# Moving the output of a fused convolution and expert kernel onto TensorE, with squares as small products and some sums on GpSimd

## The chip, the cores and the metric

One core of a Trainium2 chip runs the whole program. The metric is the device time of one execution in microseconds (us), smaller is better. The kernel before takes 186.46 us (median of 4 runs, 184.03 to 187.41). Executions of one kernel differ: the 59 of before in the set of fw_best2 took 182.97 to 194.24 us. A run is called slow here when it lies over 1.5% above the fastest of the same kernel, and fast otherwise.

Engines are named as in the profile: PE is TensorE's matmuls, PEld its weight loads, DVE is VectorE, ACT ScalarE, POOL GpSimd, SP the queue that issues most transfers.

## The reference, cut to what matters

Two residual blocks on x of 2048 tokens by 640 features (five blocks of 128 features; sixteen tiles of 128 tokens). The first is a layer norm, a short and a long convolution (by FFT), and a product. The second is a layer norm, a routing score per token, and a gated expert on the eight best tokens alone.

```python
h = layernorm(x) * (1 + ca) + sa
x = x + ga * (h * y)                  # y: the convolutions of k, v
# ---- from here on: the tail ----
h = layernorm(x) * (1 + cb) + sb      # needs mean and variance of each token's row
r = h @ w_r                           # routing score, one per token
idx = argsort(-r)[:8]                 # eight tokens
hs = h[idx]
y = (silu(hs @ w_gate) * (hs @ w_up)) @ w_down * sigmoid(r[idx])
x = x + gb * (h + scatter(y, idx))    # output: every token; the expert's part: eight
```

With z = x·s − µ·s (s the reciprocal deviation, µ the mean), the output of an ordinary token is x + z·(gb(1+cb)) + gb·sb.

## The kernel before

The whole kernel is a list of steps in a hand-written order (`ORDER`); a star behind a step's name sends its PSUM evictions to DVE instead of ACT. The steps that the change touches, cut:

```python
def t_P(b):                                  # products and sums in frequency space
    ...
    V.tensor_tensor(out=T2[:], in0=X, in1=Hi, op=ALU.mult)
    V.tensor_tensor(out=X, in0=X, in1=Hr, op=ALU.mult)
    V.tensor_tensor(out=Xr, in0=Xr, in1=T2[:, :, 1, :], op=ALU.subtract)
    V.tensor_tensor(out=Xi, in0=Xi, in1=T2[:, :, 0, :], op=ALU.add)
    ...
def t_BT(b): ...    # inverse transform on PE, evicted to U, stored to DRAM (Ud)
def t_LU(b): ...    # loaded back in another layout (uA)
def t_AT(b):        # last factor on PE, product with h, "row addition" into xq
    ...
    V.tensor_tensor(out=t, in0=ps, in1=h, op=ALU.mult)
    V.tensor_tensor(out=xq[:, :, cc], in0=xq[:, :, cc], in1=t[:], op=ALU.add)
def t_S():          # squares of feature blocks 0 to 3, on ACT
    nc.scalar.activation(out=junk, in_=xq[:, m, 0:512], func=ACT.Square, accum_out=...)
def t_BS():         # base = x + gb*sb, formed on PE with the identity
    nc.tensor.matmul(ps[:, i, :], lhsT=ident[:], rhs=gbs[:, 0:512], start=True, stop=False)
    nc.tensor.matmul(ps[:, i, :], lhsT=ident[:], rhs=xq[:, 2 * j + i, 0:512], start=False, stop=True)
    evac(base, ps)
def t_R(b):         # transposes of xq, evicted to xT, products with w_r and with ones
    ...
def t_N():          # z of each tile: 5 on DVE, 11 on ACT
    nc.scalar.activation(out=xn(m), in_=xq[:, m, :], func=ACT.Identity, scale=rs2, bias=nm2)
def t_F():          # output: two DVE instructions for a pair of tiles
    V.tensor_tensor(out=x2, in0=xn(2 * j, 2), in1=gbo, op=ALU.mult)
    V.tensor_tensor(out=x2, in0=x2, in1=base, op=ALU.add)
def t_COL():        # columns of the modulation: transposes, eleven short DVE steps,
    ...             # then a product with ones that PE waits for (near 80 us)
def t_T():          # variance, score r_bf, top 8, one-hot, selected rows xsT,
    ...             # gate, up, down, delta, scatter onto the output
```

## Time and profile before

| | before |
|---|---|
| time, median | 186.46 us |
| span of the profiled run | 183.9 us |
| last row addition into xq ends | 147.03 us |
| score r_bf ends | 156.6 us |
| selected rows xsT end | 170.3 us |
| mean granted PE clock | 0.919 |

I cut the span by three events: the last row addition, the score r_bf, the end. The stretch to the first is called the front (147.0 us), the next the score (9.6 us), the last the tail (27.3 us). Of the page, two rows matter here; each digit is a fortieth of the span, PE's busy share and PE's granted clock in tenths:

```profile
PE   0669989985989999939999969999679578165850
PEclk9999999999999999995799999999999999955555
```

PE works nearly without a stop until three quarters of the span, stops once near 80 us (the 3), and in the tail works in pieces and at half clock (the 5s).

### The profile page before, as it was taken

What the parts mean: (1) busy time and instruction counts of PE and PEld (TensorE: products, weight loads), DVE (VectorE), ACT (ScalarE), POOL (GpSimd) and SP (SyncE); (2) the same over time, 40 slices, a digit from 0 to 9 for tenths busy, and PEclk for the clock granted to TensorE, in tenths of its full rate; (3) what the DMA queues carried; (4) which work ended last, traced back from release to release, by engine and by line L of the source; (5) the groups of instructions that cost most, each with busy time, mean ns of one, the idle gap of its engine ahead of it and who ended that gap; (6) DMA issues with size and microseconds to landing.
All of it is one profiled execution on the core that took longest, in us unless ns stands there. A gap on an engine that the chain in (4) does not pass through costs nothing.

```text
span 183.9 us, 4109 instructions
## 1 busy us (share of the span) xinstructions
PE 144.0 (78%) x1664; PEld 112.5 (61%) x1664; DVE 157.7 (86%) x283; ACT 136.2 (74%) x180; POOL 33.2 (18%) x81
## 2 busy tenths in 40 slices
PE   0669989985989999939999969999679578165850
PEld 0225979952768679837679759998577342024840
DVE  5869998988979899977599999989979996999930
ACT  4368789792897979775599979999448999996000
POOL 7997500005001022010010020020200102100003
PEclk9999999999999999995799999999999999955555
DMA  6999989999999999992041999994768099705540
GB/s 108 152 204 278 313 186 326 272 198 274 265 292 320 338 304 309 176 200 114 0 171 61 212 320 324 368 338 183 200 261 224 8 293 362 310 4 219 207 153 2
DMA packets 68668, 40.68 MB, mean 221 GB/s; under 512 B 44904, under 2 KB 64808, under 8 KB 68648
## 3 DMA queue, kind: packets, MB, share of 16 engines
q1 hardware_dynamic: 65160, 35.15, 72.7%
q0 software_dynamic: 1520, 5.25, 7.7%
q10 hardware_dynamic: 1968, 0.01, 0.7%
q8 instruction: 13, 0.21, 0.5%
q14 instruction: 7, 0.06, 0.1%
HBM read 24.67 MB, written 10.50 MB: 191 GB/s over the span
## 4 chain that ended last, share of the span: by engine, by line
DVE 27%; DMA 27%; PE 24%; ACT 12%; issue 6%; SPq 2%; POOLq 1%; POOL 0%; DVEq 0%; ACTq 0%
DMA kT<-in_A_k_dram 9%; PE ps L295 8%; ACT junk L404 7%; DMA kvd<-kvT 7%; DMA uA<-Ud 6%; DVE kvT L297 4%; DVE st L581 4%; PE ps L274 3%; PE ps L314 3%; DVE xq L641 3%; DMA Ud<-U 3%; DVE xq L643 3%; PE ps L384 2%; ACT U L58 2%; ACT A L58 2%
## 5 line engine op out<-in xcount | busy, mean ns | idle before, releaser
L58 ACT CAST A<-ps 128x1024 bf16<-128x1024 f32 x35 | 33.6, 1030 | 8.5 <-PE ps L274 8.5
L58 ACT CAST HX<-ps 128x1024 bf16<-128x1024 f32 x37 | 35.9, 1054 | 2.8 <-PE ps L318 2.8
L314 PE MATMUL ps<-A,FT 128*128 128x256 bf16 x160 | 36.2, 272 | 0.4 <-DVE kvT L297 0.4
L318 PE MATMUL ps<-A,FT 128*128 128x128 bf16 x160 | 35.0, 219 | 0.0
L316 PE MATMUL ps<-A,FT 128*128 128x128 bf16 x160 | 35.0, 219 | 0.0
L295 PE MATMUL ps<-kT,dg 128*128 128x512 bf16 x80 | 21.6, 426 | 7.0 <-DMA kT<-in_A_k_dram 7.0
L58 ACT CAST U<-ps 128x1024 bf16<-128x1024 f32 x20 | 19.8, 1048 | 5.0 <-PE ps L350 2.3
L295 PEld LDWEIGHTS <-dg 128*128 128x128 bf16 x80 | 8.5, 108 | 17.4 <-issue 3.8
L354 POOL DMA_DIRECT2D Ud<-U x10 | 5.7, 572 | 72.9 <-ACT U L58 62.9
L348 PE MATMUL ps<-IT,HX 128*128 128x256 bf16 x80 | 18.1, 273 | 0.8 <-DVE kvT L297 0.8
L350 PE MATMUL ps<-IT,HX 128*128 128x256 bf16 x80 | 18.1, 273 | 0.0
L297 DVE TENSOR_TENSOR kvT<-ps,vT 128x1024 bf16<-128x1024 f32 x10 | 12.1, 1220 | 6.9 <-PE ps L295 5.7
L318 PEld LDWEIGHTS <-FT 128*128 128x128 bf16 x160 | 15.7, 98 | 1.8
L316 PEld LDWEIGHTS <-FT 128*128 128x128 bf16 x160 | 15.6, 98 | 0.9 <-issue 0.8
L314 PEld LDWEIGHTS <-FT 128*128 128x128 bf16 x160 | 15.7, 98 | 0.3
L237 POOL TENSOR_SCALAR dg<-ident,shk_f 128x128 bf16<-128x128 bf16 x16 | 10.3, 659 | 20.0 <-PE ps L295 20.0
L384 PE MATMUL ps<-RAT,uA 128*128 128x128 bf16 x160 | 10.4, 219 | 4.2 <-DMA uA<-Ud 4.2
L404 ACT ACTIVATE junk<-xq 128x512 bf16<-128x512 bf16 (+1 forms) x23 | 12.2, 533 | 2.0 <-DVE xq L391 1.3
L389 DVE TENSOR_TENSOR t<-ps,h 128x1024 bf16<-128x1024 f32 x10 | 12.2, 1218 | 1.7 <-PE ps L384 1.6
L581 DVE BATCH_NORM_STATS2 st<-xq 128x6 f32<-128x320 bf16 x32 | 13.2, 478 | 0.5 <-DMA xq<-in_A_q_dram 0.5
L274 PE MATMUL ps<-RA,gA 128*128 128x256 bf16 x80 | 12.3, 309 | 1.5 <-DVE gA L281 1.5
L333 DVE TENSOR_TENSOR HX<-HX 128x2048 bf16<-128x2048 bf16 x10 | 12.2, 1225 | 0.4
(218 smaller groups left out, 308.6 us busy)
## 6 DMA issues: line engine op xcount, KB each, us to landing
Ud<-U POOLq DMA_DIRECT2D x10, 512.0 KB, 6.0
uA<-Ud SPq DMA_DIRECT2D x10, 512.0 KB, 6.5
early<-in_w_mod_dram SPq DMA_DIRECT2D x6, 800.0 KB, 7.3
gA<-in_A_ssm_k_dram SPq DMA_DIRECT2D x5, 512.0 KB, 5.0
kvd<-kvT SPq DMA_DIRECT2D x10, 256.0 KB, 3.9
xq<-in_A_q_dram SPq DMA_DIRECT2D x4, 640.0 KB, 6.4
xA<-kvd SPq DMA_DIRECT2D x5, 512.0 KB, 4.8
out_dram<-xq SPq DMA_DIRECT2D x4, 640.0 KB, 3.1
```

Source lines behind the costliest of these rows:

```text
L58: self.nc.scalar.copy(out=out, in_=in_)
L274: nc.tensor.matmul(ps[:, bb // 2, :, (bb % 2) * 8:(bb % 2) * 8 + 8], lhsT=src[:, 4 * g4 + bb, :], rhs=RA[:].rearrange("p k c e -> p (k c) ...
L295: nc.tensor.matmul(ps[:, i, :], lhsT=diags[b][:, j, :], rhs=kT[:, n0 - j:n0 - j + 512], start=(j == 0), stop=(j == 3))
L297: V.tensor_tensor(out=kvT[:, 1024 * i2:1024 * i2 + 1024], in0=ps[:].rearrange("p a b -> p (a b)"), in1=vT[:, 1024 * i2:1024 * i2 + 1024], ...
L314: nc.tensor.matmul(ps[:, i], lhsT=FT[:, 0, k2, :], rhs=A[:, 2 * k2:2 * k2 + 2, u, :], start=True, stop=False)
L316: nc.tensor.matmul(ps[:, i, 0, :], lhsT=FT[:, 1, k2, :], rhs=A[:, 2 * k2 + 1, u, :], start=False, stop=False)
L318: nc.tensor.matmul(ps[:, i, 1, :], lhsT=FT[:, 2, k2, :], rhs=A[:, 2 * k2, u, :], start=False, stop=True)
L348: nc.tensor.matmul(ps[:, i, :], lhsT=hx[:, k2, 0, 1, :], rhs=IT[:, k2, 1:3, :].rearrange("p a b -> p (a b)"), start=True, stop=False)
L350: nc.tensor.matmul(ps[:, i, :], lhsT=hx[:, k2, 1, 1, :], rhs=IT[:, k2, 0:2, :].rearrange("p a b -> p (a b)"), start=False, stop=True)
L384: nc.tensor.matmul(o, lhsT=uA[:, bb, cs * P:(cs + 1) * P], rhs=RAT[:, cs, :].rearrange("p (m e) -> p m e", e=8), start=(cs == 0), stop=(cs ...
L404: nc.scalar.activation(out=junk()[:, 0:n], in_=xq[:, m, b0 * P:b0 * P + n], func=ACT.Square, accum_out=dst[:, m:m + 1])
L581: V.bn_stats(out=st1[:, m, hf, :], in_=xq[:, m, hf * 320:hf * 320 + 320])
```

## The change

The intent: in the tail DVE and ACT did all the output work while PE had gaps, so the output goes to PE. The transposed rows, which the score needs anyway, are kept, and the output of a tile is five products of them with diagonal matrices diag(gb(1+cb)) plus two products of four rows (mean and deviation, each in two bf16 parts, against four rows of constants). The squares of blocks 0 to 3 become 32x32 products of the transposed rows with themselves, whose diagonal is picked out. Eleven large DVE sums go to POOL, the row sum is split from its product, the inverse root has two steps fewer, and the order string is new from its first line on.

```diff
-LK0 START TC RA DIAG0 RA TAB0 RAT LG0 LK1 C0:2 ...          (ORDER, rewritten as a whole)
+LK0 START RA LG0 RA DIAG0 TAB0 LK1 TAB0 TAB1 C0:2 TC ...
...
+    def off():
+        return nc.gpsimd if evac.vector else V
...
-            V.tensor_tensor(out=Xr, in0=Xr, in1=T2[:, :, 1, :], op=ALU.subtract)
-            V.tensor_tensor(out=Xi, in0=Xi, in1=T2[:, :, 0, :], op=ALU.add)
+            off().tensor_tensor(out=Xr, in0=Xr, in1=T2[:, :, 1, :], op=ALU.subtract)
+            off().tensor_tensor(out=Xi, in0=Xi, in1=T2[:, :, 0, :], op=ALU.add)
...
-    def t_S(): ...          (squares of blocks 0 to 3 on ACT)
-    def t_BS(): ...         (base on PE; t_BL likewise)
+    def t_GR():
+        ...
+                    for b in range(4):
+                        nc.tensor.matmul(ps[t, m, :], lhsT=xTs[b][:, m, t], rhs=xTs[b][:, m, t],
+                                         start=(b == 0), stop=(b == 3), tile_position=(0, 32 * j))
...
-    def t_N(): ...          (z on DVE and ACT)
     def t_F():
-            V.tensor_tensor(out=x2, in0=xn(2 * j, 2), in1=gbo, op=ALU.mult)
-            V.tensor_tensor(out=x2, in0=x2, in1=base, op=ALU.add)
+            for b in range(NB):
+                nc.tensor.matmul(ps[:, b * P:b * P + P], lhsT=xTs[b][:, m, :], rhs=dgb[:, b, :], ...)
+            nc.tensor.matmul(ps[:, 0:512], lhsT=h_["rows"][:, m, :], rhs=st4[:, 0, 0:512], ...)
+            nc.tensor.matmul(ps[:, 512:D], lhsT=h_["rows"][:, m, :], rhs=st4[:, 0, 512:D], ...)
+            (7 tiles)  V.scalar_tensor_tensor(out=o, in0=ps[:, 0:D], scalar=rs2, in1=xq[:, m, :], ...)
+            (9 tiles)  nc.scalar.mul(out=o, in_=ps[:, 0:D], mul=rs2); V.tensor_tensor(out=o, in0=o, in1=xq, ...)
```

## The prediction

> **What bounds the kernel now.** I read the page first, then the busy time of each engine by stretches, then the chain of waits in order of time, then the groups of instructions by shape, then single stretches of the timeline. On the page no engine is alone at its limit:
>
> ```profile
> PE 144.0 (78%) x1664; PEld 112.5 (61%) x1664; DVE 157.7 (86%) x283; ACT 136.2 (74%) x180; POOL 33.2 (18%) x81
> DVE 27%; DMA 27%; PE 24%; ACT 12%; issue 6%; SPq 2%; POOLq 1%; POOL 0%; DVEq 0%; ACTq 0%
> ```
>
> The shares differ by stage, so I cut the span at events of the chain of waits: 147.0 us is the end of the last addition into the rows xq, 153.4 us the start of the variance chain, 156.6 us the routing score r_bf, 170.4 us the selected rows. The stretches (columns: length, then busy us of PE, weight load, DVE, ACT, POOL, then clock, DMA share, GB/s):
>
> ```profile
> 20.00:80.00 60.00, 54.97 (x568) 44.92 (x566) 55.13 (x95) 48.73 (x55) 7.99 (x16) 1.00 1.09 272
> 80.00:90.00 10.00, 7.20 (x30) 4.50 (x31) 6.53 (x19) 6.31 (x7) 1.08 (x4) 0.66 0.44 112
> 90.00:130.00 40.00, 37.79 (x464) 33.75 (x462) 38.31 (x46) 35.23 (x37) 3.59 (x7) 1.00 0.74 229
> 147.00:153.40 6.40, 5.00 (x48) 2.88 (x49) 5.16 (x19) 6.05 (x25) 0.25 (x2) 1.00 0.94 304
> 156.60:170.40 13.80, 5.79 (x90) 3.66 (x90) 13.21 (x35) 12.06 (x15) 0.95 (x2) 0.66 0.46 177
> 170.40:184.00 13.60, 6.41 (x212) 5.98 (x212) 5.88 (x14) 0.35 (x2) 1.56 (x1) 0.50 0.33 115
> ```
>
> From 20 to 130 us DVE is 92 to 96% busy with ACT close behind: both empty PSUM, and PE waits for them. The exception is 80 to 90 us, where PE stops and comes back at half clock. From 138.3 to 153.4 us the chain is the squares on ACT, one after another; from 156.7 us it is DVE, and then the write of the output. In the chain of waits and the groups:
>
> ```profile
> 82.61 0.14 POOL early L525
> 82.80 0.59 PE ps L527 x2
> 83.61 4.38 PE ps L274 x20
> ...
> 152.99 0.41 ACT junk L404 x2
> 153.43 0.19 DVE tot L653
> ...
> 173.59 0.75 DVE xq L641
> 175.21 3.58 DMA out_dram<-xq
> L404 ACT ACTIVATE junk<-xq 128x512 bf16<-128x512 bf16 x16 | 10.1, 630 | 1.8 <-DVE xq L391 1.3
> L643 DVE TENSOR_TENSOR xq<-xq,base 128x1280 bf16<-128x1280 bf16 x8 | 6.6, 825 | 0.3
> L391 DVE TENSOR_TENSOR xq<-xq,t 128x1024 bf16<-128x1024 bf16 x10 | 6.9, 692 | 0.3
> ```
>
> [...] the 128x16 sum on POOL (L281) took 0.26 us at 45.5 us, but 1.24 us at 68.7 us, ending just after the DVE product L333 that ran from 68.57 to 69.79 us. [...] Here PE lay idle 79.9 to 82.8 us, the clock was 0.50 to 89 us, and after the idle stretch around 159 us it stayed 0.50 to the end. [...] The trace: 1.22 us from PSUM (L389), 0.69 us from SBUF, same 1024 columns.
>
> **The change, part by part.** The order of instructions on the engines shows what moved; durations are those of before.
>
> Front, to the last addition. Five pairs of spectral sums go to POOL: DVE loses 10 x 0.69 = 6.9 us, [...]. One of ten row sums goes too, -0.7. Two of the ten products after AT are split, copy on ACT (1.05) and product in SBUF (0.69), saving 2 x 0.5 = 1.1 on DVE. Against this DVE takes two more evictions, 2 x 1.21 = +2.4. DVE: -6.3 us; ACT: two evictions fewer, two copies more, zero. About 0.7 of it counts, since PE and ACT are near their limits too: -4.5. The memset of the ones moves to the start, so PE at 80 us no longer waits for POOL, though still for the eleven DVE instructions before L527, which end at 81.9 us: about 1 us of the stop goes, and with it perhaps the half clock, which cost about half of 6.6 us. I take -2.5 for both. The three evictions of base on DVE (3 x 1.22) leave the stretch 130 to 147 us, but that stretch waits for the round trip of the last block through DRAM (eviction ends 132.6, product starts 143.4): -1.5. The last store goes through SP instead of POOL: -1. [...] Sum: -7.
>
> From the last addition to r_bf (9.6 us before). The sixteen 512-wide squares (16 x 0.75 with the read of the accumulator = 12 us) leave ACT, and the base matmuls leave PE. In their place 256 small 32x32 matmuls. The 128x8 pairs of the expert stage run one per 26.7 ns (70 in 1.87 us), so I take 27 ns: 192 before the last block's transposes = 5.2 us, 64 after = 1.7 us. PE starts them about 2.6 us before the last addition, so the transposes slip about 2.5 us; then the eviction of the fifth block 1.2, mask product and reduction 0.7 each, two small ones: the variance starts about 6 us after the last addition instead of 6.4. The inverse root has 13 instead of 15 steps of 0.21 us: -0.4. Sum: -1.
>
> From r_bf to the end (27.3 us before). Gone: five normalisations on DVE and eleven on ACT (0.83 us apart, which the selection waited for) and sixteen DVE output instructions of 0.82 us. New: sixteen 4-column transposes (0.9 us warm, 1.7 cold), their copy on ACT (as xT, 1.87 us), and for each of sixteen row tiles 1280 PE columns: 0.55 us warm, 1.07 cold. Each tile is emptied by one DVE instruction from PSUM (0.85 us, seven tiles) or by ACT (0.75) plus a DVE sum (0.49, nine tiles). The path: r_bf, rows and top-8 in parallel until about +5, two output tiles, one-hot at about +6.5, selection directly from xq without waiting for the normalised rows (80 x 27 ns), scale and shift: the selected rows at about +10.5 instead of +13.7. But then PE has ten output tiles ahead of the gate matmuls, paced by ACT at 0.75 us; gate, four tiles and up follow on the same PE. The last tile lands in SBUF at about +21, the down product ends at about +24, the output write takes 3.7, and the closing scatter and end 5.1 (178.8 to 183.9 now). That makes about 29.8, or +2.5. The tail loses on its own: output and experts now share PE, where before DVE wrote the output while PE did the experts.
>
> Sum: -7 - 1 + 2.5 = -5.5, a span of 178.4 us. The profiled run took 1.8 us more than its span and the median 2.8 more, so I add 2.3: about 180.5 us.
>
> **Rivals.** (a) The front does not shorten: POOL's sums [...] block DVE fully, and what DVE is spared comes back as blocked products; [...]. For it: L281 at 68.7 us. Against it: the pairs have other blocks' work around them. Then the front gives -2, and the time is about 186. (b) PE stays at half clock through the output: 16 x 0.5 = 8 us more on PE, perhaps 5 on the path. For it: 0.50 from 161 us on in the present tail. Against it: from the selection on PE is now dense. Time about 184. (c) The reorder is worth more than I count: with loads in order of need and no PE stop, the front loses 11 us or more; the time is 174 to 176. For it: the order string was rewritten as a whole. (d) The small matmuls cost 50 ns a pair, so that the 192 take 9.6 us: +4 before the score, about 184.
>
> **Range and chances.** (a), (b) and (d) pull up to 184 to 187, (c) down to 174; with all three terms off by two or three us in either way I take 174.5 to 186.5. Faster by over 2% means under 183.0: 0.64. Within 2%: 0.31. Slower: 0.05, since it needs two rivals at once.
>
> **What would show it.** Right: the last row addition at 140 us (134 to 144); [...] no clock loss near 80 us; the variance chain about 6 us after the last addition; selected rows 10 to 11 us after the score; from score to end 29 to 31 us, longer than now. Wrong: a last addition later than 145 us, or a tail after the score of 27 us or less (then PE and ACT overlap better than I think), or above 33 (half clock).

## The result, and the profile after

The kernel after takes 201.06 us (median of 4 runs, 198.70 to 202.84). A ratio in this text is the mean time of one kernel's fast runs over that of the other's fast runs of the same rounds, so it is not quite the ratio of the medians quoted. It is 1.075 here, 95% interval 1.053 to 1.097: slower by 7.5%. The profiled run is slow (span 201.1 us); its clock, 0.852, is close to that of the fast runs (0.859 and 0.853), and the run without POOL sums, below, has a fast profile with the same tail. The spans of the fast runs are 196.8 and 198.5 us; less a tail of 41.1 us that leaves 155.7 to 157.4 us up to r_bf, by this estimate as much as before (156.6). So the tail carries nearly the whole loss between fast runs, and the +2.4 and +1.0 of the table belong to a slow one.

| | before | after | change | predicted |
|---|---|---|---|---|
| front, to the last row addition | 147.0 | 149.4 | +2.4 | −7 |
| score, to r_bf | 9.6 | 10.5 | +1.0 | −1 |
| tail, to the end | 27.3 | 41.1 | +13.8 | +2.5 |
| span | 183.9 | 201.1 | +17.2 | −5.5 |

The same rows of the page after, with the line of busy times that answers to the one in the prediction:

```profile
PE 161.0 (80%) x2007; PEld 124.2 (62%) x2010; DVE 149.6 (74%) x269; ACT 118.5 (59%) x141; POOL 68.5 (34%) x108
PE   0779998959999997089999999956872168999980
PEclk9999999979999999859999999999699555555555
```

DVE has 8 us less to do and ACT 18 us less, and yet the span is longer. PE's row ends in 8999980 above a clock of 5: it is full and slow. The tail by stretches (length, then busy us of PE, PEld, DVE, ACT, POOL, then clock, DMA share, GB/s):

```profile
149.40:160.00 10.60, 2.85 (x113) 2.44 (x112) 7.56 (x32) 2.82 (x14) 7.59 (x11) 0.77 0.66 214
160.00:172.30 12.30, 9.23 (x125) 6.54 (x125) 6.85 (x27) 1.91 (x2) 1.40 (x4) 0.50 0.01 1
172.30:192.50 20.20, 20.20 (x217) 10.78 (x216) 8.86 (x15) 7.49 (x11) 0.00 (x0) 0.50 0.27 99
```

For 20.2 us PE is busy without a gap, and the clock is 0.50 throughout. DVE and ACT stand idle more than half of that time: PE alone is the bound. One output tile on PE, from the timeline (start, duration, engine, line, operation, partitions of operands, shapes):

```profile
181.46 0.71 PE L672 MATMUL ps<-dgb,xT 128*128 128x128 bf16 x5
182.11 0.60 PE L674 MATMUL ps<-st,rows 4*128 4x512 bf16 x1
182.51 0.31 PE L675 MATMUL ps<-st,rows 4*128 4x128 bf16 x1
182.75 0.71 PE L672 MATMUL ps<-dgb,xT 128*128 128x128 bf16 x5
```

From one tile to the next is 182.75 − 181.46 = 1.29 us, where the prediction had 0.55 warm and 1.07 cold. The cold figure was right for products that fill all 128 rows, as a tile at the same clock of 0.50 shows in a later run, fw, in which the four rows are padded with zeros to 128:

```profile
172.08 0.74 PE L675 MATMUL ps<-dgb,xT 128*128 128x128 bf16 x5
172.61 0.63 PE L677 MATMUL ps<-st,rows 128*128 128x512 bf16 x1
173.04 0.31 PE L678 MATMUL ps<-st,rows 128*128 128x128 bf16 x1
173.14 0.74 PE L675 MATMUL ps<-dgb,xT 128*128 128x128 bf16 x5
```

Here it is 173.14 − 172.08 = 1.06 us. The products last about as long; most of the 1.29 − 1.06 = 0.23 us more in after lies where the number of rows changes: from the first of five products to the 512-column one 0.65 against 0.53 us, and from the last product to the next tile 0.24 against 0.10.

Near 80 us the timeline of after shows what POOL's sums do to DVE:

```profile
79.58 0.48 DVE L507 TENSOR_TENSOR modv<-modv 128x640 bf16<-128x640 bf16 x1
79.83 2.20 POOL L361 TENSOR_TENSOR HX<-HX,T 128x1024 bf16<-128x1024 bf16 x1 [3.26 <-DVE HX L359]
79.98 2.40 DVE L508 TENSOR_TENSOR modv<-modv 128x640 bf16<-128x640 bf16 x1
82.00 2.36 POOL L362 TENSOR_TENSOR HX<-HX,T 128x1024 bf16<-128x1024 bf16 x1
...
82.68 2.02 DVE L521 TENSOR_TENSOR modv<-modv 128x640 bf16<-128x640 bf16 x1
...
86.08 0.56 PE L536 MATMUL ps<-red,onesf 128*128 128x2 f32 x2 [7.04 <-DVE junk L533]
```

Products of the same shape take 0.48 us alone and 2.40 and 2.02 us beside a POOL sum. Of the eleven POOL sums of this run ten took 2.11 to 2.49 us and one 3.19 (at 109.8 us); on DVE the same sum took 0.69 us in before. PE waits for the end of that chain, 7.0 us where before it was 2.9. The bracket gives the idle time ahead of an instruction and what ended it.

Last, PE stops twice in the middle of a group of instructions that need nothing new. From the waits of this slow profile (us in total, times, longest):

```profile
PE ps L462 <- issue: 3.4, 1, 3.4
PE ps L433 <- issue: 1.3, 1, 1.3
```

### The profile page after: what moved, and what is told of

The parts are those of the page before. It is cut to its first block, busy times and chain, and to the rows that moved or that the text cites.

```text
span 201.1 us, 4778 instructions
## 1 busy us (share of the span) xinstructions
PE 161.0 (80%) x2007; PEld 124.2 (62%) x2010; DVE 149.6 (74%) x269; ACT 118.5 (59%) x141; POOL 68.5 (34%) x108
## 5 line engine op out<-in xcount | busy, mean ns | idle before, releaser
L58 ACT CAST A<-ps 128x1024 bf16<-128x1024 f32 x34 | 32.9, 1029 | 11.7 <-PE ps L299 11.6
L58 ACT CAST HX<-ps 128x1024 bf16<-128x1024 f32 x36 | 35.0, 1041 | 3.8 <-PE ps L343 3.8
L376 PE MATMUL ps<-IT,HX 128*128 128x256 bf16 x80 | 19.2, 284 | 0.3 <-DVE HX L362 0.3
L374 PE MATMUL ps<-IT,HX 128*128 128x256 bf16 x80 | 19.3, 284 | 0.0
L380 POOL DMA_DIRECT2D Ud<-U x8 | 4.8, 604 | 41.1 <-ACT U L58 41.1
L361 POOL TENSOR_TENSOR HX<-HX,T 128x1024 bf16<-128x1024 bf16 x5 | 11.9, 2379 | 18.4 <-DVE early L253 13.0
L411 PE MATMUL ps<-RAT,uA 128*128 128x128 bf16 x160 | 10.9, 227 | 2.5 <-DMA uA<-Ud 2.5
L299 PE MATMUL ps<-RA,gA 128*128 128x256 bf16 x80 | 11.4, 291 | 1.5 <-DVE gA L306 1.5
L359 DVE TENSOR_TENSOR HX<-HX 128x2048 bf16<-128x2048 bf16 x10 | 12.3, 1230 | 0.3
L358 DVE TENSOR_TENSOR T<-HX 128x2048 bf16<-128x2048 bf16 x10 | 12.2, 1220 | 0.4
L825 POOL DMA_INDIRECT out_dram<-delta,idx x1 | 1.6, 1577 | 30.7 <-DVE delta L823 30.7
```

The costliest lines, as they stand in the source:

```text
L58: self.nc.scalar.copy(out=out, in_=in_)
L374: nc.tensor.matmul(ps[:, i, :], lhsT=hx[:, k2, 0, 1, :], rhs=IT[:, k2, 1:3, :].rearrange("p a b -> p (a b)"), start=True, stop=False)
L376: nc.tensor.matmul(ps[:, i, :], lhsT=hx[:, k2, 1, 1, :], rhs=IT[:, k2, 0:2, :].rearrange("p a b -> p (a b)"), start=False, stop=True)
L411: nc.tensor.matmul(o, lhsT=uA[:, bb, cs * P:(cs + 1) * P], rhs=RAT[:, cs, :].rearrange("p (m e) -> p m e", e=8), start=(cs == 0), stop=(cs ...
```

## The experiments

Four theories stood at the outset. **A**: PE enters the output at half clock because it idled before, and once warm it would stay warm. **B**: the output's own products cannot bring the clock back. **C**: the stops by issue are instruction fetches that stand behind the weight loads. **D**: POOL's sums cost at other places what they relieve. Later a fifth question arose, what bounds the front. All sixteen runs gave the reference's result. They were made in four sets, each on one chip against its own runs of before; times of different sets compare by their ratios. "Last addition", "r_bf" and "tail" are read in the timeline of each profiled run.

| run | time, median | ratio (95%) | last addition | r_bf | tail |
|---|---|---|---|---|---|
| after | 201.06 | 1.075 (1.053–1.097) | 149.4 | 160.0 | 41.1 |
| a_late | 200.24 | 1.075 (1.065–1.084) | 147.7 | 160.0 | 41.2 |
| a_latewarm | 198.28 | 1.071 (1.062–1.080) | 148.4 | 156.3 | 39.9 |
| a_fullrows | 191.81 | 1.031 (1.023–1.038) | 149.3 | 158.1 | 32.1 |
| a_nopool | 200.34 | 1.079 (1.070–1.087) | 147.1 | 156.0 | 41.1 |
| fw | 191.65 | 1.011 (1.004–1.019) | 147.0 | 159.2 | 32.7 |
| fw_p2v | 190.40 | 1.005 (0.999–1.011) | 149.7 | 157.6 | 32.8 |
| fw_colsplit | 190.84 | none (one fast run, 186.12) | 145.6 | 157.4 | 32.6 |
| fw_latedep | 191.22 | 1.013 (1.011–1.015) | 147.2 | 155.2 | 31.6 |
| a_oldout | 201.92 | 1.090 (1.078–1.102) | 149.6 | 160.5 | 39.2 |
| b_col | 186.05 | none (two fast runs, 185.14 and 183.29) | 145.1 | 154.5 | 28.9 |
| fw_best | 187.89 | 1.012 (1.004–1.020) | 147.9 | 155.9 | 31.8 |
| fw_rows64 | 200.55 | 1.082 (1.067–1.097) | 148.8 | 156.9 | 40.1 |
| b_newout | 205.68 | 1.103 (1.092–1.114) | 154.5 | 163.5 | 41.4 |
| b_col5 | 187.67 | 1.000 (0.995–1.004) | 146.7 | 156.6 | 27.9 |
| b_warm | 185.35 | 0.998 (0.993–1.003) | 144.8 | 154.2 | 27.9 |
| fw_best2 | 186.25 | 1.008 (1.004–1.013) | 146.9 | 154.8 | 30.8 |

The last addition moves by 1 to 2 us between profiles of kernels whose front is the same (a_fullrows and after 149.3 and 149.4, a_late 147.7), so differences of that size in that column prove nothing alone. The tail moves likewise: before, b_col and b_col5 have the same one, with 27.3, 28.9 and 27.9 us.

### a_late: the weight loads later in the order

```diff
-R3* WG AT4* ... AA4:2 WD SV ... CP:3 GR R4 T:2 Q
+R3* AT4* ... AA4:2 SV ... CP:3 GR R4 WG WD T:2 Q
```

> The changed kernel, with the loads of the up and down weights issued after the last block's transposes instead of before the small squares. Theory: PE stopped 3.4 us in the middle of the last transposes (and 1.3 us in the squares) with every operand ready, because its own instructions come by DMA and queue behind 4 MB of weights while the small matmuls use up instructions at 12 ns each. Then both stops shrink to under 0.5 us and the span loses 3 to 5 us. Rival: the fetch is limited by itself, whatever else the DMA engines do; then the stops stay and the time is within 1 us of the changed kernel.

200.24 us, as after; PE's stops by issue were 4.5 and 1.3 us. The edit turned out to be no test: with the loads later in the order the DMA share from 140 to 154 us was still 1.02 to 1.13 (0.81 to 1.16 in after), so DMA was as full beside the squares as before. Theory C was neither helped nor hurt.

### a_latewarm: PE kept busy with dummy products up to the output

```diff
+    16 products of 512 columns before the transpose of r_bf, 10 after the counting products
```

> As a_late, plus 16 idle-time matmuls of 512 columns while the variance chain runs and 10 more while the rows are copied, whose result nobody reads. Theory A: the clock fell only because PE lay idle there; kept busy it stays at 1.0 through all sixteen output tiles, a tile takes 0.55 instead of 1.29 us, and the span loses 8 to 10 us against a_late. Theory B: the output tiles themselves do not hold the clock, because half of their columns are matmuls with four rows; then it falls to 0.5 within 4 to 7 us of the first tiles though PE is 100% busy, and the gain is 2 to 4 us.

198.28 us. The stretches from 160 us on (columns as above):

```profile
160.00:164.00 4.00, 3.57 (x67) 2.36 (x65) 3.58 (x11) 0.28 (x2) 0.95 (x2) 1.00 0.01 4
164.00:168.00 4.00, 3.44 (x53) 2.53 (x49) 1.88 (x8) 0.00 (x0) 0.00 (x0) 0.54 0.02 4
...
172.00:176.00 4.00, 4.00 (x23) 1.84 (x23) 1.48 (x3) 2.52 (x4) 0.00 (x0) 0.50 0.11 41
```

The clock is 1.00 up to 164 us, so PE was warm for the first two output tiles (from 160.7 us). It fell in the selection of the rows that follows them and did not come back in the dense output after it, while PE was busy without a gap. Theory A alone falls: warming buys 2 us at most.

### a_fullrows: the four rows padded with zeros to 128

```diff
-st4 = const.tile([4, 2, D], BF)              # constants of the rank one products
+st4 = const.tile([P, 2, D], BF)              # partitions 4 to 127 set to zero
-rows = ring.tile([4, M, P], BF)
+rows = ring.tile([P, M, P], BF)              # likewise
```

> The changed kernel, with the rank-one rows padded by zeros from 4 to 128 partitions, so that the 512 and 128 column matmuls of each output tile span all rows of the array at the same number of columns. Theory B: the clock comes back to 1.0 within 7 us of 171 us and the span loses 5 to 8 us. Theory A (what counts is only whether PE has instructions): the clock stays at 0.50 to the end, as in the changed kernel, and the span is within 1 us.

191.81 us, 8 to 9 us less than after, with the same number of products of the same number of columns. The clock was back at about 172 us, and the tail is 32.1 us, 9 us less:

```profile
172.00:176.00 4.00, 3.95 (x50) 3.02 (x50) 2.45 (x5) 3.42 (x6) 0.00 (x0) 0.96 0.46 168
```

Theory B holds: what kept the clock down was the four-row form of the products. Not shown is what in that form does it. The few rows are one candidate; the time lost at each change of the number of rows, which the padding removes too, is the other, and no run takes them apart. The profile shows no gap there, but it models the ends of the products.

### a_nopool: the eleven sums back on DVE

```diff
-            off().tensor_tensor(out=Xr, ...)          (and Xi, and the row sum)
+            V.tensor_tensor(out=Xr, ...)
```

> The changed kernel, with the eleven large sums taken back from GpSimd to DVE and nothing else changed. Theory: the sums on GpSimd hold up DVE at the wrong place: two products on modv (0.48 us) return from 2.40 and 2.02 us, the stop of PE near 80 us falls from 7.0 us to 3 or 4, half clock after it shrinks or goes, and the last row addition comes 3 to 5 us earlier. Rival: DVE's relief was worth its price; without it DVE is 7 us busier before the last addition and this comes 0 to 3 us later.

200.34 us against 201.06: no difference. The products on modv take 0.48 us again and PE's stop near 80 us is 4.4 us instead of 7.0, so the blocking is as theory D has it. But the time stays, so POOL's part is worth about nothing in either direction. The run also bears on the order string, which was never put back alone: with the new order and no POOL sums the last addition is at 147.1 us, where before had 147.03, so the new order by itself brought no 7 us either. The tail is 41.1 us in this fast profile, exactly as in the slow one of after.

### fw: full rows and dummies together

```diff
+    the edits of a_fullrows and a_latewarm
```

> Full rows and warm dummies together: the rank one rows padded with zeros from 4 to 128 partitions, 16 + 10 dummy products of 512 columns around the score, as in the runs before that had one of the two each (191.8 us and 198.3 us). Theory B (the clock is at half when the output begins and products of four rows cannot bring it back): neither part alone is enough, since padding alone still starts the output cold (clock 1.0 only from 172 us) and warming alone is lost again at 164-168 us. Together the clock should be 1.00 from about 146 us to the end of the products, an output tile should take 0.55-0.65 us from the first one, and the time should be 185-188 us. Rival (each gives its gain for another reason and they overlap): 190-192 us, and the clock falls again in the output.

191.65 us, ratio 1.011. By the numbers that is the rival's outcome (190 to 192 us, and a second fall of the clock), though the fall lay in the selection of the rows, after the first two tiles. The clock was not 1.00 to the end:

```profile
164.00:168.00 4.00, 3.38 (x67) 2.43 (x66) 3.39 (x10) 0.00 (x0) 0.62 (x2) 1.00 0.02 4
168.00:172.00 4.00, 3.31 (x49) 2.90 (x50) 2.06 (x8) 0.00 (x0) 0.00 (x0) 0.57 0.02 4
172.00:176.00 4.00, 4.00 (x32) 3.06 (x31) 2.01 (x4) 2.06 (x3) 0.00 (x0) 0.58 0.44 164
176.00:180.00 4.00, 3.95 (x101) 3.53 (x100) 2.69 (x6) 3.74 (x6) 0.00 (x0) 1.00 0.40 148
```

It fell at 169 us, after eight us with PE busy 3.2 to 3.4 us in four, and came back at 175 us in the dense output. In a_latewarm the same fall was final. That is theory B a second time: the dense output brings the clock back with 128 rows and not with four. It also shows that A's half is real: with these gaps a stretch at half clock followed, and with PE busy 3.95 us in four (fw_best2, below) none did up to 176 us.

### fw_p2v and fw_colsplit: the stop near 80 us

```diff
 fw_p2v:       -... G4:2 P2* OG G3 COL ...          the pair of POOL sums beside the columns on DVE
               +... G4:2 P2 OG G3 COL ...
 fw_colsplit:  -... P2 OG G3 COL H:4 G3 BT1:4       and the column step cut before its last products
               +... P2 OG G3 COL BT1:2 H:2 COL H:2 G3 BT1:2
```

> As fw, with one step of the eleven large GpSimd sums taken back to VectorE: the two sums (128x1024) that run beside the column products near 80 us. Theory (the relief of VectorE is given back there, because the products on modv take 2.40 and 2.02 us beside GpSimd instead of 0.48, and PE waits for their chain): the PE stop near 80 us falls from 7.0 to 4.4-5 us, and the last row addition comes 1.5-3 us earlier than in fw, so 183-186 us. Rival (GpSimd sums cost VectorE about what they relieve, everywhere, not there alone): no more than 0.7 us.

> As fw_p2v, and the step with the column products is cut in two: PE gets two steps of the inverse transform (BT of block 1) between the transposes and the product with ones that waits for VectorE's chain of eleven short operations. If that wait is on the path that sets the time of the last row addition, PE's stop near 80 us falls from 4-5 us to under 1 us, the half clock behind it (some 7 us in every kernel so far) goes away, and the last addition comes 3-6 us earlier: 179-183 us. If VectorE alone sets that time, PE's stop is free slack and the time is within 1 us of fw_p2v.

PE's stop fell from 5.9 us (fw) to 4.9 and to 2.1 us, and in fw_colsplit the clock between 80 and 90 us rose from 0.66 to 0.90. The times were 190.40 and 190.84 us; of before (17 of 23), fw_p2v (15 of 21) and fw_colsplit (3 of 4) most runs were slow, and fw_colsplit had one fast run (186.12). The last addition came later in fw_p2v than in fw (149.7 against 147.0) and earlier in fw_colsplit (145.6). No clear gain; the question goes on with b_col.

### fw_latedep: the weight loads made to wait

```diff
+    V.tensor_copy(out=wu[:, 0, 0:1], in_=xTs[4][:, 15, 0:1])     (and wd: overwritten by the load)
```

> As fw, and the loads of the up and down weights cannot begin before the last transposed rows are out of PSUM (a copy of one column into their tiles, overwritten by the load). Theory C (the stops of PE by issue of 0.8-4.5 us around the small squares are the fetch of instructions beside weight loads): DMA share between 140 and 155 us falls from about 1.0 to under 0.6, and the stops by issue fall under 0.5 us together. Rival D (the burst of about 75 products a us is itself faster than instructions arrive): the stops stay at 1.5 us or more. Time 0-2 us below fw under C, equal to fw or up to 3 us above under D (loads end later).

This is the test that a_late was not. The stretch around the squares, first fw, then fw_latedep (columns as above), and fw_latedep's only stop by issue there:

```profile
142.00:150.00 8.00, 5.70 (x244) 5.24 (x243) 6.03 (x18) 3.80 (x15) 2.82 (x4) 0.83 1.02 368
```

```profile
142.00:150.00 8.00, 6.14 (x317) 5.58 (x314) 6.52 (x19) 3.55 (x14) 0.99 (x3) 0.96 0.01 2
```

```profile
PE ps L465 <- issue: 0.5, 1, 0.5
```

The DMA share falls from 1.02 to 0.01 and the stops from 5.5 to 0.5 us. But fw's profile is of a slow run and this one of a fast. Among fast profiles the stops are 1.8 to 2.5 us with the loads beside the squares (a_latewarm, a_fullrows, a_nopool, fw_rows64) and 0 to 0.7 without (fw_latedep, fw_best, fw_best2): that the loads cause most of them is shown, at about 2 us. From the last addition to r_bf it is 7.9 us instead of 12.2 in fw, but a_latewarm, fast and with the loads, has 7.9 too, so no gain of the score is shown. That what PE waits for are its instructions is inferred: the list of queues in the page of after has one for them (packets, MB, share of 16 engines), and no trace shows a fetch held up:

```profile
q8 instruction: 15, 0.25, 0.6%
```

The time is the same within the interval (1.013 against 1.011). Whether the loads, which now begin at 152.5 us and run beside the tail, take something back, the runs do not tell.

### a_oldout: the output put back, a failed test

```diff
-... GR CP GR:2 R3 R4* CP:3 GR R4 T:2 Q T F* T F* ...
+... GR BS:2 GR:2 R3 R4* GR R4 T BS:4 BL N:5 N* T N* N* N:2 T N N* N:3 N* F T F:3 BL F T:2 F:3 T:4
```

> The kernel after, with the output alone formed as in the kernel before (base on TensorE during the row additions, ScalarE and VectorE scaling the rows, two sums on VectorE); the order ahead of it, the GpSimd sums and the small squares stay. If the output on TensorE at half clock is what lost the tail, the time from r_bf to the end falls from 41.1 us to 27-30 us and the kernel takes 186-190 us (what is left over before is the front, some 2 us, and the stops by issue). Rival (the loss is in the new score and selection steps, which stay): 195 us or more.

201.92 us, and by the letter of what was expected the rival won. I had put the second half of the base products behind the score's own steps, so that the transpose of r_bf began at 163.9 us, 3.4 us after r_bf; and the new selection has a copy on ACT and two steps on DVE that waited behind the normalisations (until 170.6 us) and the output sums (until 181.2 us). The order, not the output, made this tail.

### fw_rows64: half the rows

```diff
-st4, rows: 128 partitions (fw)
+st4, rows: 64 partitions
```

> As fw, with the rank one rows padded to 64 partitions and not to 128. If the granted clock follows how much of the array's rows work on average, the output's share is (640*128+640*64)/(1280*128), three quarters, and the clock comes back to 1.00 in the output, perhaps later than in fw (some 6 us after it fell); if every product has to fill more than half of the rows, it stays at 0.50 to the end of the output, as with four rows, and the time is 195-198 us.

200.55 us, where 195 to 198 was expected, tail 40.1 us. PE was as dense as in fw, and the clock fell at about 165 us and stayed:

```profile
164.00:168.00 4.00, 3.45 (x74) 2.75 (x70) 2.12 (x9) 0.00 (x0) 0.00 (x0) 0.56 0.00 0
...
176.00:180.00 4.00, 4.00 (x28) 1.86 (x29) 1.52 (x4) 2.48 (x4) 0.00 (x0) 0.50 0.44 164
```

So 64 rows are not enough when half of the columns are of that kind, and 128 are. Where between them the limit lies, and whether it is the rows, their share of the work or the change from one number of rows to another (from 172 to 176 us PE ran 24 products here, 25 in after and 32 in fw, so by this estimate that time is lost as with four rows), is not measured.

### b_col and b_col5: the stop near 80 us mended in the kernel before

```diff
-    onesf = early[:, 9728:9984]; nc.gpsimd.memset(onesf, 1.0)      (in the column step)
+    onesf set at the start; yield before the product with ones
-... BT1 COL G3:2 H:3 G3 ...
+... BT1 COL G3:2 H COL H:2 G3 ...
```

> The kernel before, with two edits at the column products alone: the ones for the sum over partitions are set at the start, and PE gets two evictions' worth of products (G of block 3) between the transposes and the product with ones. If PE's stop near 80 us (2.9 us, and half clock for 6.6 us after it) is on the path that sets the last row addition, as the prediction had it (2.5 us of its 7), the time is 183-184.5 us where the kernel before has 186; if not (the stop is slack that VectorE's or the loads' order takes anyway), within 0.7 us of before.

> The same kernel as b_col, for the interval: 0.7-1.5 % faster than before (1.3-2.8 us) if the stop near 80 us with its half clock is on the path of the last addition (in b_col's profile that came 1.9 us earlier); within 0.4 % if b_col's two fast times were luck.

In b_col the clock from 80 to 90 us is 1.00 instead of 0.66, and the last spectral sum ends at 127.3 us instead of 129.3 (126.1 in b_col5). That is the 2 to 3 us that the prediction gave this stop. But the time did not follow: the first two fast times looked 0.9% better, and with eight fast runs against those of before the ratio is 0.9996. The gain is lost between the last spectral sum and the score. The timeline of b_col5 shows where in that run; first before, then b_col5, the last eviction of U (on its way to DRAM) and the first product that uses it:

```profile
130.62 1.93 ACT L58 CAST U<-ps 128x1024 bf16<-128x1024 f32 x2 [1.54 <-issue]
...
141.64 1.07 PE L384 MATMUL ps<-RAT,uA 128*128 128x128 bf16 x16
```

```profile
127.40 1.93 ACT L58 CAST U<-ps 128x1024 bf16<-128x1024 f32 x2 [1.54 <-issue]
...
141.12 1.95 PE L386 MATMUL ps<-RAT,uA 128*128 128x128 bf16 x32
```

The eviction is 3.2 us earlier, the product 0.5 us. The way through DRAM took 9.1 us before and 11.8 here; it was 9.0 in b_col. In other profiles it took 11.1 us (after), 9.2 (a_nopool), 9.8 (fw_colsplit) and 9.5 (fw_best2). They do not settle what sets it.

### fw_best and fw_best2: all repairs, and the last fall of the clock

```diff
 fw_best:   fw_latedep, a_nopool and the column cut together
 fw_best2:  + 4 dummy products before the one-hot, 5 before the selection of rows
```

> All repairs together: full rows, dummies, the late dependency of the weight loads, the eleven sums back on VectorE, and the column step cut in two. From fw_latedep (188.8-191.3 us, all repairs of the tail) the front should gain what fw_colsplit and the kernel without GpSimd sums showed: last addition at 144.5-146 us, and 184.5-187.5 us in all: no better than the kernel before by more than 1 %, since r_bf to the end is still 31-32 us where the kernel before has 27.3. If it comes out under 183 us, the change pays once its clock and its waits are mended.

> fw_best with 9 more dummy products around the selection of the rows, where its clock fell at 164 us and came back only at 171 us. If the clock is all that is left over of the tail's loss, it stays at 1.00 to the last product, r_bf to the end falls from 31.8 us to 28-29.5 us (29.8 was the estimate on record), and the time is 184-186 us against fw_best's 187.2-189.5. If the clock falls again nevertheless, within 0.7 us of fw_best.

fw_best takes 187.89 us; its clock fell at 164 us and came back at 171 us. In fw_best2 it stayed:

```profile
164.00:168.00 4.00, 3.95 (x103) 3.60 (x102) 2.27 (x9) 0.00 (x0) 0.00 (x0) 1.00 0.49 159
168.00:172.00 4.00, 3.95 (x60) 3.17 (x58) 3.23 (x7) 3.90 (x6) 0.00 (x0) 1.00 0.46 168
```

A tile takes 0.55 us from one to the next, as predicted for a warm PE; the tail is 30.8 us where the prediction had 29.8, and where 28 to 29.5 was expected for this run. The dummies are part of it: the transpose of r_bf, first step to the selection, begins 1.6 us after r_bf here and 0.4 us in before. It takes 186.25 us, ratio 1.008 (1.004 to 1.013), within 2% of before, and still not faster.

### b_newout: the output part alone, put into the kernel before

```diff
 before's order up to the score, squares on ACT, all sums on DVE
-... R2* BS*:2 R2 ... T BS:2 BL N:5 ... F T:3 ...
+... CP:5 ... T:2 Q T F* T F* T F*:2 F:8 T F*:3 F T:4
```

> The kernel before with the output part of the change alone (transposed rows kept, diagonals and rank one rows of four partitions on TensorE, new selection of rows); its own order up to the score, its own squares on ScalarE, no GpSimd sums, no repair. The earlier attempt at the reverse (a_oldout) was spoilt by the order I gave it. If the output alone carries the loss of the tail, the last addition stays at 146-148 us, r_bf to the end is 39-42 us (27.3 before, 41.1 after), clock 0.50 throughout the output, and the time is 195-200 us. Rival (the tail of after is slow because of what its order and squares do ahead of it): r_bf to the end 28-32 us, 186-189 us.

205.68 us, tail 41.4 us at a clock of 0.50 to the end (27.3 before, 41.1 after). The output alone carries the loss of the tail; neither the small squares nor POOL nor the new order is needed for it. Its front is 7.5 us longer than that of before (last addition at 154.5 us): PE waited 8.3 us for the loads of uA there, and the time as a whole is beyond what I expected. My estimate of the cause, not shown: the change moved the last store of U from POOL's queue to SP's, where the loads of uA are issued too. In before SP issues two loads of uA from 128.4 us; in after, with the same move, it issues stores of U at 127.5 and 132.5 us and loads of uA at 130.3 and 138.4. The prediction counted the moved store as −1. So this run holds a little more than the output part, though nothing more in the tail.

### b_warm: dummies in the tail of the kernel before

```diff
+    b_col with some 35 dummy products in PE's gaps between r_bf and the down products
```

> b_col with some 35 dummy products of 512 columns in PE's gaps between the score and the end, where b_col ran at 0.50 from 157 us on. Clock 1.00 through the selection and the projections; the three projections take 1.0-1.4 us each instead of 2.0, but the up product waits for VectorE's last output sums (until 173.3 us in b_col), so only the down projection and the last step gain: 1-2 us below b_col5, 182-184 us. If the dummies stand in the way of the selection, equal to b_col5 or up to 1 us above.

185.35 us, ratio 0.998: not faster than before. The clock was 1.00 from 156 to 167 us, fell to 0.50 from 169 to 175 us in spite of the dummies. From r_bf to the selected rows it is 13.9 us (13.7 before), from there to the product of gate and up 5.0 us (5.0 before): there PE is not the bound, and a warm clock gains nothing. The last step is 1.2 us longer (4.5 against 3.3 us), so the six dummies ahead of the down product stood in its way. No version beat both kernels.

## Why the prediction was wrong

**The tail, +2.5 put down, +13.8 found: the largest error, and its cause is shown.** The step that failed is the rejection of rival (b), "Against it: from the selection on PE is now dense", and with it the warm term of 0.55 us for a tile. PE was dense and stayed at half clock. The work was counted right: with 128 rows and no gap (fw_best2) a tile takes 0.55 us and the tail 30.8 us, so the mechanism "The tail loses on its own: output and experts now share PE" holds with +3.5, of which the dummies' own time is a part (1.2 us more ahead of the transpose of r_bf than in before). The mis-sized term is a tile on PE: 1.29 us and not 0.55. Of the 0.74 us lost, 0.51 is the half clock (1.06 for full rows at 0.50) and 0.23 the change between four rows and 128; over sixteen tiles the latter makes an estimate of 3.7 us. Between the tails, 41.1 − 30.8 = 10.3 us, 9.0 came back by padding alone (a_fullrows), which mends both, and 1.2 by dummies alone (a_latewarm). Rival (b) itself was sized at +5, since it had the cold tile at 1.07 us.

**The front, −7 put down, +2.4 found in a slow profile** (fast ones of the same front, with POOL's sums, give +0.2 to +2.3: fw_latedep, a_latewarm, fw_rows64, a_fullrows). The failed step is "About 0.7 of it counts, since PE and ACT are near their limits too: −4.5". DVE was relieved: its busy time up to the last addition went from 130.8 to 125.1 us. But its idle time went from 16.2 to 24.3 us, and the last spectral sum ended at 129.4 us, before at 129.3. A high busy share with short waits did not make DVE the bound (these figures are of the slow profile; the fast run a_nopool, where DVE is not relieved, has its last addition at 147.1 us, no later than the relieved ones). The second term, −2.5 for PE's stop near 80 us, had the wrong sign, since the stop grew from 2.9 to 7.0 us: the contention of DVE and POOL, for which the sum of −7 holds +2.5, an estimate of mine spread evenly over DVE's time and not measured before, shows in DVE's timeline in one place, at the chain that PE waits for (2.40 and 2.02 us for 0.48). And even taken away it brings no time (b_col5, 0.9996). The third and fourth terms (−1.5 and −1, around the last block's way through DRAM) did not appear either: from the last eviction of U to the first product of that block it is 9.1 us before and 11.1 after. What bounds the front is not settled. Shown is that neither DVE's load, nor POOL's sums (a_nopool), nor PE's stop does so alone. That the last 15 us of it hang on a DRAM round trip of 9 to 12 us is read from the traces (before 9.1, b_col 9.0, b_col5 11.8); no run changed that trip alone. The cause stays open. Rival (a), "what DVE is spared comes back as blocked products", saw the contention rightly but not as the cause: without POOL the time is the same.

**The score, −1 put down, +1.0 found in the slow profile, −0.7 to −1.7 in the seven fast ones** (fw_rows64, a_latewarm, a_fullrows, a_nopool, fw_latedep, fw_best, fw_best2). So the sum came true where the state is the same, but partly by luck. The small products run at 9.5 ns each (192 in 1.83 us, fw_latedep) and not at 27, so the 192 were done before the last addition. Against this, two stops by issue came in, which no rival had: 4.7 us together in the slow profile of after, 1.8 to 2.5 in fast ones.

**The rivals together.** I gave slower than 2% a chance of 0.05, "since it needs two rivals at once". One was enough: (b) at its true size. A slip without effect: 178.4 + 2.3 is 180.7, where the text has about 180.5.

**What held**: the score's −1 in fast profiles, selected rows early (12.3 us after r_bf against 13.7 before, at half clock; 10 to 11 put down), tile counts and the two marks for "wrong", a last addition after 145 us and a tail above 33 us, both of which came.

## What to carry to other kernels

When work moves to PE, look at the rows that each product fills and not only at its columns. A product of a few rows took as long here as one of 128 (0.60 against 0.63 us for 512 columns at half clock), the change from 128 rows to four and back cost 0.23 us a tile, and a gapless PE stayed at half clock (0.50 for 20.2 us in after); padding with zeros took all of that away (a tile 1.06 us at 0.50, and the clock back to 1.00 in a_fullrows) and brought 9 us back. An engine that is 95% busy (DVE in before, 92 to 96% from 20 to 130 us) is not thereby the bound: take the relief into a single event further down (here the last spectral sum) before counting it. Bulk loads beside hundreds of tiny products made PE stop here, by about 2 us (1.8 to 2.5 in fast profiles); moving the loads took the stops away (0 to 0.7 us), but did not change the time.
